# A fused long convolution and token MLP on one core: the filter's transposes into 16-bit PSUM, and another fixed order

## The chip, the core and the metric

The kernel runs on one core of one Trainium2 chip. The metric is the device time of one execution in microseconds; the times shown are medians of several runs. A profile is one execution recorded by the hardware, with its own time.

## What is computed

The reference, cut to what matters (D = 640 channels, S = 2048 steps, F = 1536; all tensors bf16):

```python
def _A_ref(q, k, v, shift_k, ssm_k, ssm_D):          # long convolution
    k_shift = sum of k shifted by 0..3 steps, times shift_k per channel
    kv = k_shift * v
    y = causal convolution of kv with ssm_k along S   # by FFT of length 2S
    y = y + kv * ssm_D
    return q * y
def _B_ref(x, w1, b1, w2, b2):                        # MLP over the steps
    u = gelu(einsum("bsd,sf->bdf", layernorm(x), w1) + b1)
    return transpose(einsum("bdf,fs->bds", u, w2) + b2)
g = sigmoid((q * gate_w).sum(-1))
return g * _A_ref(...) + (1 - g) * _B_ref(q, ...)
```

## The kernel before

**The work.** The convolution is done with matrices of cosines and sines. The filter `ssm` is five blocks of 128 channels by 2048 steps; it is loaded block by block (`db` = 0 to 4). For each half `h` of the steps and each block, `transp` (L798) transposes eight 128x128 pieces on TensorE, by multiplying with the identity `ident`, into one PSUM slot, and one instruction copies the slot, scaled by 1/1024, into `wT`. So there are ten such blocks of eight transposes. For `h` = 0, GpSimd first adds the channel's `ssm_D` to the filter's first step (L803). Then `wblock` (L818) multiplies `wT` with the tables FE, FN and FO into the filter's spectrum: two groups of 16 matmuls of 128 columns per block, each group evacuated by one instruction ("Wb") into C. FE and FN are computed on the core; FO is loaded in two tables of 256 KB (p = 1 and p = 3). For `h` = 1 every group reads both FO tables; for `h` = 0 one of the two groups reads them.

Beside that, `x_load` brings q (as X) in pieces; VectorE takes its statistics (L897), GpSimd works out the reciprocal deviation (L902), and ScalarE or VectorE normalizes X in 16 instructions (L911). k is permuted by VectorE (`k_turn`, L702) and transposed by DMA into KT, multiplied by the shift filter KF on TensorE ("kv"), and by v on VectorE. Then come the spectrum of kv ("A"), the first MLP matmul ("m1", 12 tiles of four groups of eight matmuls of 320 columns, reading X and the weights in `ring`), the products of the spectra on VectorE, the second MLP matmul ("m2", reading GT and W2), and the inverse transform ("inv", reading C or SS and GTB). The last TensorE group is an m2 group; two VectorE instructions (L627) and an output DMA follow it.

**PSUM slots.** There are four slots (`pp`) of 1024 float32 per partition. Each group of matmuls has one, and the group that gets the slot next has to wait for its evacuation. The kernel's own tracker (class `_Tracker`) writes a semaphore wait for every overlap of memory.

**The order.** Every operation has a number in the order in which the code creates it (0 to 648). `_ORDER` (L1318) lists all numbers in the order in which they are issued; each engine's queue is that list cut to its own operations, and each engine works strictly in that order. `_ENG` (L1342) has one letter for each of the 50 operations that may go to ScalarE ("A") or VectorE ("D"): for each block one wT and two Wb, the 16 normalizations, and the four permutations of k. `_SLOTS` (L1343) gives the PSUM slot of each group. Nothing of that is worked out when the kernel runs.

The numbers that are used below:

| number | operation |
|---|---|
| 2; 5 | load of filter block 0, first half; second half |
| 6, 7, 8, 9 | loads of filter blocks 1 to 4, 512 KB each |
| 3, 4 | load of X, first 512 rows: 160 KB and 480 KB |
| 12, 13, 14 | loads of the other three parts of X, 640 KB each |
| 10, 11 | loads of the two FO tables, 256 KB each |
| 15, 16, 17 | small loads of b2 and b1 |
| 18, 19, 45, 46 | loads of W1's first third, by part of the rows |
| 43, 44 | loads of k, first half |
| 36, 38 | ScalarE: the sine of the tables; a gelu of one element that brings the gelu table |
| 60, 67, 74, 81, 88 | GpSimd: addition of `ssm_D` for blocks 0 to 4 |
| 61, 68, 75, 82, 89 | TensorE: transposes for h = 0, blocks 0 to 4; the evacuations are 62, 69, 76, 83, 90 |
| 197, 203, 209, 215, 221 | the same for h = 1; the evacuations are 198, 204, 210, 216, 222 |
| 63, 70, 77, 84, 91 and 65, 72, 79, 86, 93 | TensorE: spectrum groups of h = 0 without and with FO |
| 199 to 225 in steps (199, 201, 205, 207, ...) | TensorE: spectrum groups of h = 1 |
| 53 to 59 | TensorE: dummy pairs of matmuls on zeros (`zz`), 512 columns |
| 131 to 134, 152 to 155, 173 to 180 | normalizations of X, four per part |
| 181 to 184 | GpSimd: the four products that make KF |
| 186, 188, 241, 243 | SP: DMA transposes of k |
| 405 | ScalarE: the gelu of the fifth m1 tile |
| 482, 483, 484, 501 | loads into W2 where m2 groups have read it (483 waits for 479, its first user is 519) |
| 611, 612 | VectorE: the last two operations that write SS |

The queues around the change, before. SP: 13, 6, 2, 7, 10, 11, 14, 17, 8, 12, 4, 44, 9, 43, 3, 5, 18, then the DMA transposes 188 and 186. TensorE: 55, 53, 57, 59, 56, the small constants (48), 54, then 203, 68, 58, 61, 209, 75, 207, 65, 79, 72, 211, 82, and so on. ScalarE: the sine, then evacuations; 38 stands behind 405. VectorE takes wT of 61 and 75 (62 and 76) and two of the Wb.

Of the kernel before, what the change touches and what calls it, by code (L numbers as in the profile page):

```python
# [9 lines left out]
BF16 = mybir.dt.bfloat16  # L10
# [9 lines left out]
class _Tracker:  # L20
# [265 lines left out]
    def mm(self, ps_ap, lhsT, rhs, start, stop, final_val, inc, transpose=False):  # L286
        acc_r = []
        for a in (lhsT, rhs):
            for r in self.regions(a):
                acc_r.append((r, "R"))  # L290
        acc = list(acc_r)
        ps_regs = self.regions(ps_ap)
        if start:
            for r in ps_regs:
                acc.append((r, "W"))
        need = self.deps_for("PE", acc)
        self.do_waits("PE", need)
        ins = self.nc.tensor.matmul(ps_ap, lhsT=lhsT, rhs=rhs, start=start, stop=stop, skip_group_check=True)  # L298
        src = ("eng", "PE", final_val)
        for reg, mode in acc_r:  # L300
            self.add_record(reg, "R", src)
        for r in ps_regs:
            self.add_record(r, "W", src)
        if inc:
            ins.then_inc(self.clk["PE"], 1)
            self.cnt["PE"] += 1
            assert self.cnt["PE"] == final_val, (self.cnt["PE"], final_val)
            self.hist["PE"].append(dict(self.known["PE"]))
        return ins
# [123 lines left out]
def _build(nc, A_q, A_k, A_v, A_shift_k, A_ssm_k, A_ssm_D, B_x, B_w1, B_b1, B_w2, B_b2, gate_w, out):  # L433
    Bsz, S, D = A_q.shape
# [5 lines left out]
    SL = 4 * D  # L440
# [3 lines left out]
    with ExitStack() as es:  # L444
        clk = {e: es.enter_context(nc.semaphore(f"clk_{e}")) for e in ENGS}
        T = _Tracker(nc, clk)

        pp = []
        for i in range(4):
            h = es.enter_context(nc.psum_tensor(f"pp{i}", [128, 1024], F32))  # L450
# [7 lines left out]
        def alloc(name, shape, dtype, at=None):  # L458
            size = mybir.dt.size(dtype)
            for s_ in shape[1:]:  # L460
                size *= s_
            if at is None:
                off = cur[0]
                cur[0] = (off + size + 63) // 64 * 64
            else:
                off = at
            assert off % 4 == 0 and off + size <= top, f"SBUF overflow {name}: {off}+{size} > {top}"
            h = nc.alloc_sbuf_tensor_at(name, list(shape), dtype, offset=off)
            T.reg_sbuf(h, off)
            return h  # L470

        def base_of(h):
            return T.mem[h.name][1]

        def V(h, off, dims, p0=0, pn=128):
            row = T.mem[h.name][2]
            return bass.AP(tensor=h, offset=p0 * row + off, ap=[[row, pn]] + [list(d) for d in dims])

        gwb = alloc("gwb", [128, D], BF16)
        ident = alloc("ident", [128, 128], BF16)  # L480
# [40 lines left out]
        ssm = alloc("ssm", [128, ND, S], BF16, at=base_of(C[3]))  # L521
        wT = alloc("wT", [128, 4, 4, D], BF16, at=base_of(C[2]))
# [82 lines left out]
        def either(name, o, i, rd, on_act, on_dve, vt=None):  # L605
            e_ = {"A": "ACT", "D": "DVE"}[next(which)]

            def emit(s):
                src = i(s) if vt is not None else i
                return T.op(e_, lambda e: (on_act if e_ == "ACT" else on_dve)(e, src), rd + [src], [o])  # L610
            return SC.add(e_, act_dur(n_of(o)) if e_ == "ACT" else dve_dur(n_of(o), 1), emit, rd if vt is not None else rd + [i], [o], vt=vt, name=name)

        def evac(name, o, i, vt, scale=1.0):
            kw = {} if scale == 1.0 else {"scale": scale}
            return either(name, o, i, [], lambda e, src: e.activation(o, src, ACT.Copy, **kw),  # L615
                          lambda e, src: e.tensor_copy(o, src) if scale == 1.0 else e.tensor_scalar(o, src, scale, None, op0=ALU.mult), vt=vt)
# [18 lines left out]
        def memset(eng, ap, val, prio=None):  # L635
            return nolock(eng, 0.2, lambda s: T.op(eng, lambda e: e.memset(ap, val), [], [ap]), [], [ap], prio=prio)

        def mms(vt, items, prio=None, name="mm"):
            dur = sum(max(n_of(r) / 2400.0 + 0.0025, 0.056) for _, _, r, _, _ in items)
            rd = []  # L640
            for _, l, r, _, _ in items:
                rd += [l, r]

            def emit(s):
                fv = T.cnt["PE"] + 1
                for k_, (o, l, r, st, sp) in enumerate(items):
                    T.mm(o(s), l, r, st, sp, fv, k_ == len(items) - 1)
            return SC.add("PE", dur, emit, rd, [], prio=prio, vt=vt, name=name)

        ndma = [0]  # L650
# [129 lines left out]
        vt = _VT("cv")  # L780
        items = []
# [16 lines left out]
        def transp(h, db):  # L798
            vt = _VT("cv")
            items = []  # L800
            if h == 0:
                w0 = V(ssm, db * S, [[1, 1]])
                tt("POOL", w0, w0, dcol[:, db:db + 1], ALU.add)  # L803
            for j in range(7, -1, -1):
                items.append(((lambda s, j=j: s[:, 128 * j:128 * j + 128]), V(ssm, db * S + 1024 * h + j, [[8, 128]]), ident[:, :], True, True))
            m_ = mms(vt, items, name="wtr")
            evac("wT", V(wT, 2 * h * SL + 128 * db, [[SL, 2], [D, 4], [1, 128]]), (lambda s: s[:, :].rearrange("q (a b c) -> q a b c", a=2, b=4)), vt, 1.0 / 1024.0)

        def table(p, kt, c, k2):
            if p % 2:  # L810
# [245 lines left out]
        for ft in range(FT):  # L1056
# [3 lines left out]
            vt = _VT("mlp")  # L1060
            r = ring[(ft // 4) % 2]
            col = 128 * (ft % 4)
            for hk in range(4):
                items = []
# [43 lines left out]
        for hk, p in [(hk, p) for hk in range(2) for p in range(4)] + [(hk, p) for p in INVP[1] for hk in (2, 3)]:  # L1108
            for a in {(1, 0): (4, 6, 8), (2, INVP[1][0]): (10,)}.get((hk, p), ()):
                w2_pair(a)  # L1110
            vt = _VT("mlp")
# [4 lines left out]
            for a in range(na):  # L1116
                items = []
# [198 lines left out]


_ORDER = """  # L1318
# [22 lines left out]
"""  # L1341
_ENG = "DAAAAADDAAAAAADDDDDAAADDDADDDDADDAAAAAAAAAAAAAAADD"  # L1342
_SLOTS = "1120021323201331122022011133001030332021001010110220110131230121002123231321103301332230032032101133201012203121332133113300113"  # L1343
# [1 line left out]
_INS = ['A_q', 'A_k', 'A_v', 'A_shift_k', 'A_ssm_k', 'A_ssm_D', 'B_x', 'B_w1', 'B_b1', 'B_w2', 'B_b2', 'gate_w']  # L1345
_OUTS = [((1, 2048, 640), 'bfloat16')]
# [23 lines left out]
```

## Time and profile before

| what | us |
|---|---|
| median of 3 runs | 176.82 (176.80 to 177.04) |
| the profiled execution, its own time | 177.12 |
| its span, first to last instruction | 175.1 |
| TensorE (PE) matmuls busy | 170.0 |
| VectorE (DVE) busy | 168.9 |
| ScalarE (ACT) busy | 107.6 |

The page gives busy time per engine, then the span in 40 slices of 4.4 us, where each digit is the busy share of a slice in tenths. PEclk is the granted share of TensorE's clock. PEld is TensorE's loading of weights, which overlaps the matmuls. A row of a group reads: line, engine, operation, output <- inputs, shape, count, then busy time in us, mean of one in ns, and the idle time of the engine just before them with what ended it. A row of a timeline reads: start in us, length in us, engine, line, operation, output <- inputs, count, and in brackets the idle time before it and who ended it. SPq and POOLq are the DMA queues of SyncE and GpSimd; "to landing" is the time from a DMA's issue to its last byte. Matmuls overlap, so the time per matmul is read from start to start, not from the length of one. A row of stretches reads: the stretch, its length, busy time (and count) of PE, PEld, DVE, ACT and POOL, the granted clock, the DMA share and the GB/s.

### The profile page before, as it was taken

How to read it: one execution, taken by the hardware profiler on the slowest of the kernel's cores; microseconds unless marked ns; L12 is line 12 of the kernel's file. 1: busy time of each engine (PE TensorE's matmuls, PEld its weight loads, DVE VectorE, ACT ScalarE, POOL GpSimd, SP SyncE). 2: the span in 40 equal slices, each digit the busy share in tenths (PEclk: the TensorE clock that was granted, in tenths of full speed). 3: DMA queues.
4: the chain of work that ended last, by engine and by line, in shares of the span. 5: the costliest groups of instructions: out<-in, count | busy, mean ns of one | idle time of the engine just before them, and what ended most of it. 6: DMA issues, size and time to landing. Idle time of an engine off the chain costs nothing.

```text
span 175.1 us, 3683 instructions
## 1 busy us (share of the span) xinstructions
PE 170.0 (97%) x1559; PEld 138.2 (79%) x1559; DVE 168.9 (96%) x187; ACT 107.6 (61%) x160; POOL 42.7 (24%) x62
## 2 busy tenths in 40 slices
PE   7999999999899999999999999999999999999992
PEld 2599999877697767777777778888899998698782
DVE  7899999999999999999999999999999999999984
ACT  4499999997999997877556214222215105645760
POOL 3199891000000650003202202220055000052200
PEclk9999999999999999999999999999999999999999
DMA  5999999999999799992999999999939999549598
GB/s 144 397 421 405 376 200 225 380 375 221 179 383 356 172 192 192 186 358 57 178 174 365 353 211 349 282 207 240 300 108 187 197 177 372 241 65 209 106 233 292
DMA packets 33248, 44.06 MB, mean 252 GB/s; under 512 B 12112, under 2 KB 24656, under 8 KB 33104
## 3 DMA queue, kind: packets, MB, share of 16 engines
q1 hardware_dynamic: 28024, 32.68, 57.6%
q0 software_dynamic: 5168, 11.14, 37.4%
q8 instruction: 12, 0.20, 0.4%
q14 instruction: 4, 0.03, 0.1%
q10 hardware_dynamic: 40, 0.01, 0.0%
HBM read 27.44 MB, written 2.62 MB: 172 GB/s over the span
## 4 chain that ended last, share of the span: by engine, by line
PE 93%; DMA 3%; ACT 2%; DVE 0%; DVEq 0%; SPq 0%; issue 0%
PE pp L298 93%; DMA ssm<-in_A_ssm_k_dram 3%; ACT L600 1%; ACT ksh L600 1%; ACT GT L600 0%; DVE O L627 0%; DVEq L426 0%; SPq L272 0%
## 5 line engine op out<-in xcount | busy, mean ns | idle before, releaser
L298 PE MATMUL pp<-X,ring 128*128 128x320 bf16 x384 | 55.4, 299 | 0.5 <-ACT GT L600 0.5
L556 DVE TENSOR_TENSOR C<-C 128x2560 bf16<-128x2560 bf16 (+2 forms) x38 | 54.6, 1485 | 0.3 <-ACT C L600 0.2
L298 PE MATMUL pp<-GT,W 128*128 128x320 bf16 x384 | 53.6, 299 | 0.0
L298 PEld LDWEIGHTS pp<-GT,W 128*128 128x128 bf16 x384 | 48.0, 129 | 4.6
L298 PEld LDWEIGHTS pp<-X,ring 128*128 128x128 bf16 x384 | 37.0, 98 | 15.0 <-ACT GT L600 0.8
L600 ACT ACTIVATE O<-pp,c,omg 128x640 bf16<-128x640 f32 x15 | 12.9, 883 | 24.8 <-PE pp L298 24.8
L267 POOL DMA_DIRECT2D C<-C x8 | 10.5, 1674 | 51.1 <-DVE C L556 30.0
L600 ACT ACTIVATE C<-pp 128x640 bf16<-128x640 f32 x32 | 20.4, 711 | 2.0 <-PE pp L298 2.0
L600 ACT ACTIVATE cgb<-pp,gg 128x640 bf16<-128x640 f32 x16 | 12.1, 795 | 13.3 <-PE pp L298 7.6
L615 ACT ACTIVATE C<-pp 128x1024 bf16<-128x1024 f32 x18 | 17.1, 1051 | 0.3 <-PE pp L298 0.3
L600 ACT ACTIVATE gq<-gq 128x640 bf16<-128x640 bf16 x16 | 11.6, 727 | 5.7 <-DVE gq L556 5.7
L556 DVE TENSOR_TENSOR tm<-C,C 128x5120 bf16<-128x5120 bf16 x5 | 14.1, 2819 | 0.1
L897 DVE BATCH_NORM_STATS2 stats<-X 128x6 f32<-128x320 bf16 x32 | 13.1, 470 | 0.4 <-DMA X<-in_A_q_dram 0.2
L298 PE MATMUL pp<-wT,FO 128*128 128x128 bf16 x160 | 12.4, 219 | 0.0
L600 ACT ACTIVATE GT<-pp,cc 128x640 bf16<-128x640 f32 x12 | 9.3, 793 | 4.8 <-PE pp L298 4.7
L298 PE MATMUL pp<-C,GTB 128*128 128x320 bf16 x80 | 11.9, 299 | 0.0
L298 PE MATMUL pp<-wT,FE 128*128 128x128 bf16 x120 | 11.7, 219 | 0.0
L556 DVE TENSOR_TENSOR SS<-C 128x2560 bf16<-128x2560 bf16 x8 | 11.7, 1482 | 0.0
L267 POOL DMA_DIRECT2D O<-q_hi x4 | 4.8, 1324 | 27.7 <-DVE q_hi L556 27.7
L600 ACT ACTIVATE ksh<-pp 128x1024 bf16<-128x1024 f32 (+1 forms) x12 | 10.1, 908 | 1.4 <-PE pp L298 1.3
L267 POOL DMA_DIRECT2D C<-q_hi x4 | 4.8, 1198 | 23.8 <-DVE q_hi L556 10.9
L556 DVE TENSOR_TENSOR C<-tm 128x2560 bf16<-128x2560 bf16 x7 | 10.3, 1487 | 0.1
(92 smaller groups left out, 225.3 us busy)
## 6 DMA issues: line engine op xcount, KB each, us to landing
ring<-in_B_w_dram SPq DMA_DIRECT2D x12, 512.0 KB, 8.8
W<-in_B_w_dram SPq DMA_DIRECT2D x12, 512.0 KB, 6.8
C<-C POOLq DMA_DIRECT2D x8, 640.0 KB, 8.8
kn<-in_A_k_dram SPq DMA_DIRECT2D x4, 640.0 KB, 9.6
C<-q_hi POOLq DMA_DIRECT2D x4, 640.0 KB, 9.7
out_dram<-O SPq DMA_DIRECT2D x7, 320.0 KB, 3.2
ssm<-in_A_ssm_k_dram SPq DMA_DIRECT2D x4, 512.0 KB, 7.0
X<-in_A_q_dram SPq DMA_DIRECT2D x3, 640.0 KB, 7.3
```

What stands on the lines that cost most here:

```text
L267: ins = engobj.dma_start(out_ap, in_ap, accum_op=ALU.add, max_dma_last_dim=2560)
L298: ins = self.nc.tensor.matmul(ps_ap, lhsT=lhsT, rhs=rhs, start=start, stop=stop, skip_group_check=True)
L556: o_ = SC.add(eng, d, lambda s: T.op(eng, lambda e: e.tensor_tensor(o, a, b, op), rd, [o]), rd, [o], prio=prio, name="tt")
L600: return T.op("ACT", lambda e: e.activation(o, src, func, **kw), rr + [src], ww)
L615: return either(name, o, i, [], lambda e, src: e.activation(o, src, ACT.Copy, **kw), lambda e, src: e.tensor_copy(o, src) if scale == 1.0 ...
L897: ops.append(SC.add("DVE", 0.38, (lambda o, i: lambda s: T.op("DVE", lambda e: e.bn_stats(o, i), [i], [o]))(o, i), [i], [o]))
```

## The change

Three things change. First, the transposes are issued in TensorE's transpose form (`is_transpose`), and their output is written as bf16 into the first half of the slot instead of as float32 into all of it; the evacuation reads it as bf16. Second, `_ENG` gives other operations to VectorE: wT of 68, 89 and 197 (69, 90, 198) instead of 62 and 76, nine normalizations instead of eleven, and two Wb as before (92 and 214 instead of 78 and 94). Third, `_ORDER` and `_SLOTS` are new from end to end. In the new order SP issues 12, 6, 2, 7, 13, 8, 14, 4, 10, 11, 9, 5, 44, 3, 43, 17, 18, 19, then 188 and 186; TensorE goes 58, 53, 59, 55, 56, 48, 54, then 203, 61, 68, 57, 209, 75, 63, 70, 82, 77, 215, 84, 207, 217, 211, 89, 86, 65, 221, 197, 72, 205, 201, 91, 93, 79, and so on; 38 stands right behind 36 on ScalarE.

```diff
         need = self.deps_for("PE", acc)
         self.do_waits("PE", need)
-        ins = self.nc.tensor.matmul(ps_ap, lhsT=lhsT, rhs=rhs, start=start, stop=stop, skip_group_check=True)
+        ins = self.nc.tensor.matmul(ps_ap, lhsT=lhsT, rhs=rhs, start=start, stop=stop, skip_group_check=True, **({"is_transpose": True} if transpose else {}))
...
-        def mms(vt, items, prio=None, name="mm"):
+        def mms(vt, items, prio=None, name="mm", transpose=False):
...
-                    T.mm(o(s), l, r, st, sp, fv, k_ == len(items) - 1)
+                    T.mm(o(s), l, r, st, sp, fv, k_ == len(items) - 1, transpose)
...
             for j in range(7, -1, -1):
-                items.append(((lambda s, j=j: s[:, 128 * j:128 * j + 128]), V(ssm, db * S + 1024 * h + j, [[8, 128]]), ident[:, :], True, True))
-            m_ = mms(vt, items, name="wtr")
-            evac("wT", V(wT, 2 * h * SL + 128 * db, [[SL, 2], [D, 4], [1, 128]]), (lambda s: s[:, :].rearrange("q (a b c) -> q a b c", a=2, b=4)), vt, 1.0 / 1024.0)
+                items.append(((lambda s, j=j: s[:, 64 * j:64 * j + 64].bitcast(BF16)), V(ssm, db * S + 1024 * h + j, [[8, 128]]), ident[:, :], True, True))
+            m_ = mms(vt, items, name="wtr", transpose=True)
+            evac("wT", V(wT, 2 * h * SL + 128 * db, [[SL, 2], [D, 4], [1, 128]]), (lambda s: s[:, 0:512].bitcast(BF16).rearrange("q (a b c) -> q a b c", a=2, b=4)), vt, 1.0 / 1024.0)
...
-_ENG = "DAAAAADDAAAAAADDDDDAAADDDADDDDADDAAAAAAAAAAAAAAADD"
+_ENG = "AAADAAAAAAAADDADDAADDDDDADDAAAADDDAAAAAAADAAAAAADD"
-_SLOTS = "1120021323201331122022011133001030332021001010110220110131230121002123231321103301332230032032101133201012203121332133113300113"
+_SLOTS = "1123020201110022333022012033103321113030300332311313200003131123201303300332031012002121033213031202331213200321323013131201012"
```

The 16 lines of `_ORDER` are left out; the parts of it that matter here are told above.

44 rows, old and new, of the table _ORDER are left out of this document.

## The prediction

> **What bounds the kernel now.** I read the page first, then the chain of waits in order of time, then the timelines of TensorE, VectorE, ScalarE and the SP queue. The page's busy rows:
>
> ```profile
> PE 170.0 (97%) x1559; PEld 138.2 (79%) x1559; DVE 168.9 (96%) x187; ACT 107.6 (61%) x160; POOL 42.7 (24%) x62
> ACT  4499999997999997877556214222215105645760
> PEclk9999999999999999999999999999999999999999
> ```
>
> TensorE and VectorE are both full; ScalarE is full in slices 2 to 9, about 9 to 44 us, where the change sits. The chain, in order of time (start, length):
>
> ```profile
> 1.19 5.37 DMA ssm<-in_A_ssm_k_dram
> 6.60 27.17 PE pp L298 x443
> 33.78 7.29 PE pp L298 x88
> 41.09 1.02 ACT ksh L600
> 42.13 1.28 ACT L600
> 43.43 0.81 ACT GT L600
> 44.28 127.63 PE pp L298 x988
> ```
>
> After the first filter load, TensorE runs to 171.9 us almost without a break. So I price everything by how far it delays TensorE's stream. Three stretches show its pace and its gaps:
>
> ```profile
> 10.27 3.07 PE L298 MATMUL pp<-wT,FO 128*128 128x128 bf16 x52
> 13.18 0.33 PE L298 MATMUL pp<-wT,FE 128*128 128x128 bf16 x3
> ...
> 24.74 1.21 PE L298 MATMUL pp<-ident,ssm 128*128 128x128 bf16 x16
> 25.79 0.33 PE L298 MATMUL pp<-wT,FE 128*128 128x128 bf16 x3
> ...
> 30.26 1.25 PE L298 MATMUL pp<-X,ring 128*128 128x320 bf16 x8
> ...
> 32.52 1.25 PE L298 MATMUL pp<-X,ring 128*128 128x320 bf16 x8
> 33.78 1.75 PE L298 MATMUL pp<-KF,KT 128*128 128x128 bf16 x32
> ```
> ```profile
> 40.89 1.25 PE L298 MATMUL pp<-X,ring 128*128 128x320 bf16 x8
> 41.98 0.71 PE L298 MATMUL pp<-vkv,FE 128*128 128x320 bf16 x4
> 42.52 1.25 PE L298 MATMUL pp<-X,ring 128*128 128x320 bf16 x8
> 44.28 1.26 PE L298 MATMUL pp<-X,ring 128*128 128x320 bf16 x8 [0.51 <-ACT GT L600]
> ```
>
> Start to start, a filter-spectrum matmul takes (13.18-10.27)/52 = 56 ns, so a group of 16 takes 0.89 us; a transpose (25.79-24.74)/16 = 66 ns, a block of eight 0.53; eight of 320 columns take 1.09 (40.89 to 41.98). Eight of these took 1.26 at 32.52 and 1.76 at 42.52: gaps of 0.17 and 0.67 us, behind ScalarE (the last chain rows: an evacuation, a table load, a gelu). VectorE is as tight near the end:
>
> ```profile
> 161.20 2.88 DVE L556 TENSOR_TENSOR SS<-C 128x2560 bf16<-128x2560 bf16 x2
> ```
> ```profile
> 164.12 4.51 PE L298 MATMUL pp<-SS,GTB 128*128 128x320 bf16 x32
> ```
>
> VectorE finishes SS at 164.08; TensorE needs it at 164.12. A gain therefore has to be had on both.
>
> **The change, part by part.**
>
> *Evacuations.* The rows that price them (view by shapes; the fourth is a 16-bit operation of 1024 elements per partition that reads SBUF):
>
> ```profile
> L615 ACT ACTIVATE wT<-pp 128x1024 bf16<-128x1024 f32 x8 | 8.1, 1042 | 1.1 <-PE pp L298 1.1
> L616 DVE TENSOR_SCALAR wT<-pp 128x1024 bf16<-128x1024 f32 x2 | 2.4, 1182 | 0.0
> L915 DVE TENSOR_SCALAR X<-X,rstd,nb 128x640 bf16<-128x640 bf16 x11 | 4.3, 434 | 0.0
> L570 DVE TENSOR_SCALAR pint<-pint 128x1024 int16<-128x1024 int16 x1 | 0.4, 428 | 0.0
> ```
>
> Read letter by letter, the new engine string gives VectorE three of the ten wT evacuations (two before), nine of the sixteen normalizations (eleven before), and again two of the twenty Wb. An evacuation from 16-bit PSUM is not in the trace. On VectorE it lies between 428 and 1182 ns; I take 0.7 us, between the two, as it shares the element type with the one row and the source with the other. VectorE's sum is then 3 x 0.7 - 2 x 1.18 - 2 x 0.43 = -1.1 us (+0.3 at the upper end). On ScalarE I leave 1042. [...]
>
> *ScalarE.* It loses a wT evacuation and gains two normalizations, and the second table load moves from behind op 405's place in the list to right behind the sine:
>
> ```profile
> 5.93 0.18 ACT L600 ACTIVATE dcol<-pp 128x5 bf16<-128x5 f32 x1 [1.20 <-PE pp L298]
> ...
> 27.32 4.70 ACT L615 ACTIVATE C<-pp 128x1024 bf16<-128x1024 f32 x5
> ...
> 34.03 1.79 ACT L914 ACTIVATE X<-X,nb,rstd 128x640 bf16<-128x640 bf16 x2
> ```
>
> In a row, an evacuation costs (4.70-1.05)/4 = 0.91 us and a normalization 1.79-0.98 = 0.81. So ScalarE reaches the first gelu 0.91 - 1.62 + 1.28 = 0.57 us sooner. The load falls into the 1.20 us for which ScalarE idles before 5.93; with its one-element gelu it exceeds that by 0.3 us, hidden because the filter load lands later (6.56). The gaps of 0.17 and 0.67 go: **-0.84 us**. What could be late next there is op 133, a normalization that the first MLP group needs. It stands behind 23 evacuations and one normalization: 23 x 0.91 + 2 x 0.81 = 22.6 us after the first evacuation can start (7.1, after eight transposes), so 29.7 at the least, while TensorE comes at 6.60 + 23.66 (as before, 30.26 - 6.60) + 0.53 (below) = 30.8. That hides it.
>
> *The transposes on TensorE.* 80 instructions of unchanged size. Their 66 ns against 56 may vanish (-0.8 us in all) or grow by as much; nothing in the trace decides, so zero, and 0.8 to both sides.
>
> *First transposes.* Before, the order was 203, 68, a dummy pair, then 61; now 61 comes second. 61 needs GpSimd's addition into block 0:
>
> ```profile
> 7.28 0.20 POOL L556 TENSOR_TENSOR ssm<-ssm,dcol 128x1 bf16<-128x1 bf16 x1 [0.33 <-DMA ssm<-in_A_ssm_k_dram]
> ```
>
> That ends at 7.48, and the load before it keeps its place (third, same bytes ahead). TensorE is there at 6.60 + 0.53 = 7.13: **+0.38 us**, with 68 and the dummies queued behind it.
>
> *The FO tables.* SP issued them fifth and sixth; now they are ninth and tenth, behind two more pieces of X of 640 KB, one of 480 KB and one more filter block. Issue rows, then the time from issue to landing of FO, of the 640 KB piece of X issued at 5.51 and of the 480 KB piece issued at 5.99:
>
> ```profile
> 2.75 1.30 SPq L272 DMA_DIRECT2D FO<-odd_tab  x2
> ...
> 5.51 0.96 SPq L272 DMA_DIRECT2D X<-in_A_q_dram  x2
> ```
> ```profile
> DMA to landing us min/median/max: 6.4/6.4/6.4
> ```
> ```profile
> DMA to landing us min/median/max: 8.8/8.8/8.8
> ```
> ```profile
> DMA to landing us min/median/max: 10.7/10.7/10.7
> ```
>
> Before, FO landed at 9.2 and 9.9. In the new order 4704 KB are in the queue up to the second table; the old order has the same big transfers up to the X piece that landed at 5.99 + 10.7 = 16.7 us. The 640 KB piece, with 4224 KB, landed at 14.3; the remaining 480 KB at the stretch's 406 GB/s would give 15.5:
>
> ```profile
> 4.00:14.00 10.00, 9.82 (x135) 7.95 (x134) 8.95 (x25) 7.34 (x10) 5.83 (x9) 1.00 1.02 406
> ```
>
> So the second table lands between 15.5 and 16.7. I take 16.3, near the row with the same bytes, less some for the small load of b1 that no longer stands ahead. Who needs it: group 207, the thirteenth from the first transpose in the new TensorE list. Ahead of it stand seven transposes (7 x 0.53), one dummy pair (0.43) and four spectrum groups (4 x 0.89): 6.60 + 7.7 + 0.38 = 14.7. Its last four matmuls read the second table at 14.7 + 12 x 0.056 = 15.3. **+1.0 us** (0.2 to 1.4), and all of TensorE's queue is behind it; ScalarE has evacuations in stock then, but runs dry later and cannot give it back.
>
> *Smaller waits.* By the new list and 0.91 us per evacuation TensorE meets a slot that is still being read, or the fifth block's addition behind the four KF products, a few times by under 0.1 us: **+0.15**.
>
> *The rest of the order* I cost at nothing: each later SP load has 11 us or more of TensorE work between its last reader and its first user, more than most landings of W, but for one (a rival below). SP's transposes of k and the v loads behind them start later by about the same as their users.
>
> Sum: -0.84 + 0.38 + 1.0 + 0.15 = **+0.7 us**. VectorE, 1.1 us ahead, does not bind; the tail behind TensorE's last group is unchanged. The profiled execution took 177.12 us (span 175.1 and 2.0 around it), 0.3 above the median of 176.82. So 176.82 + 0.7 = **177.5 us**.
>
> **The rivals.**
>
> *Not slower: FO lands in time.* The term decides from 15.3 us on; at 15.5 the sum falls to -0.1, **176.7**. For it: the steady 406 GB/s. Against: the last piece of the same set took until 16.7.
>
> *Faster: the transposes shed their 10 ns*, and FO lands early: -0.1 - 0.8 at best, **175.9 to 176.4**. For it: only transposes, with their strided weights, run above 56 ns. Against: the weights stay strided, and part of the gain would fall into waits for ScalarE.
>
> *Slower: VectorE gets nothing from 16 bits* (1.18 us). Place: op 198, the third of its evacuations, which 201 needs. VectorE comes to it behind 31 of the 32 statistics, a copy of k and two evacuations; I put its end at about 23 us with 0.7 each and 24.4 with 1.18, against TensorE's 23.8 with the waits above. It decides from about 1.0 us per evacuation; a further +0.5 to 1.2, **178.0 to 178.7**.
>
> [...]
>
> *A W2 load comes late.* Load 483 waits for 479, and 519 needs it six groups later, 6 x 1.09 = 6.5 us; the least room before was 10.9. Landings of all W loads, and of the one issued alone at 116.5 us:
>
> ```profile
> DMA to landing us min/median/max: 3.8/6.8/11.3
> ```
> ```profile
> DMA to landing us min/median/max: 4.7/4.7/4.7
> ```
>
> Up to +1 at the median with its issue, **178.5**; 483 would be issued nearly alone, and 4.7 hides it.
>
> **Chances.** Forecast (+0.2 to +1.4) 0.46; FO in time 0.18; faster 0.16; VectorE slow 0.09; clock 0.04; W2 or another load 0.07. About 0.2% (0.35 us) is what a measurement of this kernel tells from no change. Of FO in time 0.05 is faster by more than that, and 0.08 of the forecast lies within it: faster 0.21, same 0.21, slower 0.58. The range, 176.1 to 178.9, takes in both ends of the FO term, half of the transposes' 0.8 and the slow VectorE; the forecast's own is 177.0 to 178.2.
>
> **What would show it.** Right: a TensorE gap near 15 us released by FO, a smaller one at 7.1 by GpSimd's addition, no gap at 42 to 44, a table load before 6 us, wT evacuations on VectorE near 0.7 us. Wrong: no wait for FO; transposes at another pace; TensorE's MLP starting before 30.8 us; a granted clock below 1.0; gaps after 45 us.

## The result, and the profile after

The changed kernel took 178.73 us (median of 4 runs, 178.41 to 178.80), the kernel before 176.93 on the same chip: a ratio of 1.0093 (95% interval 1.0081 to 1.0105), 1.8 us slower. The forecast was 177.5 with a range of 176.1 to 178.9, and slower as the likeliest. The profiled execution of after took 178.74 us (before 177.12).

The page of after: busy time, then two of its rows of 40 slices.

```profile
PE 169.4 (96%) x1559; PEld 138.2 (78%) x1559; DVE 167.8 (95%) x186; ACT 109.4 (62%) x161; POOL 41.8 (24%) x62
PE   6996999999999999999999999999999999999992
PEclk9999999999999999999999999999999999999999
```

TensorE now has a hole in its fourth slice (13.2 to 17.7 us); the granted clock is 9 (90% or more) in every slice and 1.00 as the mean of each of the four runs. VectorE has 1.1 us less work than before, which is what the forecast said, and it did not help. The chain of after in order of time (start, length; short pieces left out):

```profile
4.85 11.64 DMA FO<-odd_tab
...
16.54 85.86 PE pp L298 x893
...
102.41 0.02 SPq L199
...
102.46 0.37 SPq L272
...
104.89 7.57 DMA W<-in_B_w_dram
...
112.51 55.63 PE pp L298 x408
```

Before, TensorE ran from 6.6 us to the end with one break near 43. Now the end hangs on two loads: FO, and a W2 load behind SP. The timeline of TensorE has both, and a third, smaller wait near 7:

```profile
7.07 1.20 PE L298 MATMUL pp<-ident,ssm 128*128 128x128 bf16 x16 [0.24 <-DMA ssm<-in_A_ssm_k_dram]
...
14.56 0.22 PE L298 MATMUL pp<-wT,FN 128*128 128x128 bf16 x1
16.54 0.40 PE L298 MATMUL pp<-wT,FO 128*128 128x128 bf16 x4 [1.76 <-DMA FO<-odd_tab]
...
21.35 1.17 PE L298 MATMUL pp<-ident,ssm 128*128 128x128 bf16 x16
22.35 1.06 PE L298 MATMUL pp<-wT,FO 128*128 128x128 bf16 x16
...
32.39 3.42 PE L298 MATMUL pp<-X,ring 128*128 128x320 bf16 x24
...
109.82 2.34 PE L298 MATMUL pp<-GT,W 128*128 128x320 bf16 x16
112.51 1.69 PE L298 MATMUL pp<-GT,W 128*128 128x320 bf16 x11 [0.35 <-DMA W<-in_B_w_dram]
```

Start to start, and less the matmul itself, the waits are 0.41 us at 6.6, 0.26 at 11.3 (filter block 3), 1.92 at 14.6 (FO) and 0.51 at 111.9 (W2). The gaps of 0.17 and 0.67 us behind ScalarE are gone. For the larger the reason is the table load, which stands early now (first line). The smaller had another: before, it ended with an evacuation into `ksh`, which stands ahead of the table load in ScalarE's queue (second line, TensorE's weight loads before).

```profile
5.34 1.28 ACT L600 ACT_TABLE_LOAD   x1
```
```profile
33.77 1.59 PEld L298 LDWEIGHTS pp<-KF,KT 128*128 128x128 bf16 x32 [0.34 <-ACT ksh L600]
```

A book with two entries holds it all. The first MLP matmul starts at 32.39 us (before 30.26): the start lost **2.13**. From there to TensorE's last matmul (173.56, before 171.90) it is 141.17 us (before 141.64): the rest gained **0.47**. Together that is 1.66, and the profiled executions differ by 1.62.

### The profile page after: what moved, and what is told of

Same layout as the page of the kernel before. It is cut to its first block, busy times and chain, and to the rows that moved or that the text cites. A ratio compares the mean times of both kernels' runs of the same rounds, so it can differ in the third digit from the quotient of the medians.

```text
span 176.8 us, 3679 instructions
## 1 busy us (share of the span) xinstructions
PE 169.4 (96%) x1559; PEld 138.2 (78%) x1559; DVE 167.8 (95%) x186; ACT 109.4 (62%) x161; POOL 41.8 (24%) x62
## 3 DMA queue, kind: packets, MB, share of 16 engines
HBM read 27.44 MB, written 2.62 MB: 170 GB/s over the span
## 4 chain that ended last, share of the span: by engine, by line
PE 80%; DMA 11%; SPq 3%; DVE 2%; ACT 1%; issue 0%; DVEq 0%
PE pp L298 80%; DMA FO<-odd_tab 7%; DMA W<-in_B_w_dram 4%; SPq L272 3%; DVE O L556 1%; DVE cgb L556 1%; ACT cgb L600 1%; DVE O L627 0%; DVEq L426 0%; DVE cgb L570 0%; SPq L199 0%
## 5 line engine op out<-in xcount | busy, mean ns | idle before, releaser
L600 ACT ACTIVATE O<-pp,c,omg 128x640 bf16<-128x640 f32 x15 | 13.2, 884 | 31.2 <-PE pp L298 31.2
L615 ACT ACTIVATE C<-pp 128x1024 bf16<-128x1024 f32 x18 | 17.7, 1025 | 1.6 <-PE pp L298 1.6
L897 DVE BATCH_NORM_STATS2 stats<-X 128x6 f32<-128x320 bf16 x32 | 13.7, 466 | 1.1 <-DMA X<-in_A_q_dram 1.1
L267 POOL DMA_DIRECT2D C<-SS x3 | 5.3, 1768 | 37.0 <-DVE C L556 37.0
L298 PEld LDWEIGHTS pp<-wT,FO 128*128 128x128 bf16 x160 | 9.8, 98 | 2.0 <-DMA FO<-odd_tab 1.9
L556 DVE TENSOR_TENSOR C<-tm 128x2560 bf16<-128x2560 bf16 x7 | 10.3, 1488 | 0.1
```

What stands on the lines that cost most here:

```text
L267: ins = engobj.dma_start(out_ap, in_ap, accum_op=ALU.add, max_dma_last_dim=2560)
L556: o_ = SC.add(eng, d, lambda s: T.op(eng, lambda e: e.tensor_tensor(o, a, b, op), rd, [o]), rd, [o], prio=prio, name="tt")
L600: return T.op("ACT", lambda e: e.activation(o, src, func, **kw), rr + [src], ww)
L897: ops.append(SC.add("DVE", 0.38, (lambda o, i: lambda s: T.op("DVE", lambda e: e.bn_stats(o, i), [i], [o]))(o, i), [i], [o]))
```

## The experiments

Each ratio is to the kernel before, run on the same chip, where its median was 176.89 to 177.31 us; the changed kernel's is 1.0093, and comparisons with the changed kernel go by these ratios. "SP" lines are the order of the loads in SP's queue.

### FO ahead of two pieces of X

```diff
 SP: 12 6 2 7 13 8
+10 11
 14 4
-10 11
 9 5 44
```

> Only the two FO loads move: on SP they go from ninth and tenth to seventh and eighth, ahead of two pieces of X (640 and 480 KB). Theory (FO's place in the queue makes the 1.92 us gap before group 207): the FO tables land near 12.5 us, two full pieces sooner, and the gap goes. But TensorE then reaches the fifth filter block's transposes (op 89), four groups later, at about 17.3 us, and block 4 still lands at 18.3: a new gap of about 1.0 us, so a gain of about 0.9 us against the changed kernel, near 177.8. Rival (the whole gap is recovered or kept elsewhere, because TensorE is held by ScalarE or VectorE later anyway): less than 0.3 us of gain, and the lost time shows as PSUM-slot waits after 20 us.

Measured: 179.43 us, ratio 1.0143 (1.0124 to 1.0162). FO landed at 12.5 and 13.1 and no group waits for it. TensorE, then two lines of VectorE:

```profile
18.64 0.71 PE L298 MATMUL pp<-ident,ssm 128*128 128x128 bf16 x8 [1.12 <-DMA ssm<-in_A_ssm_k_dram]
...
22.49 0.69 PE L298 MATMUL pp<-ident,ssm 128*128 128x128 bf16 x8 [0.87 <-DVE wT L616]
```
```profile
14.72 1.28 DVE L897 BATCH_NORM_STATS2 stats<-X 128x6 f32<-128x320 bf16 x3 [1.30 <-DMA X<-in_A_q_dram]
...
17.34 2.06 DVE L897 BATCH_NORM_STATS2 stats<-X 128x6 f32<-128x320 bf16 x5 [0.88 <-DMA X<-in_A_q_dram]
...
21.71 0.64 DVE L616 TENSOR_SCALAR wT<-pp 128x1024 bf16<-128x1024 bf16 x1
```

The new wait for block 4 came as expected (1.28 us start to start). Neither theory had the second one: VectorE waits twice for the pieces of X, so its evacuation of wT, queued behind 29 of the 32 statistics, is late, and TensorE waits another 1.03 us for the slot. Giving evacuations to VectorE tied TensorE to the arrival of X. The first MLP matmul starts at 33.33, later than in the changed kernel.

### FO and block 4 ahead

```diff
 SP: 12 6 2 7 13 8
+10 11
 14
+9
 4
-10 11 9
 5 44
```

> As the run before, and filter block 4 goes ahead of the 480 KB piece of X as well. Theory (each load's place decides): neither FO nor block 4 is waited for by more than 0.3 us, the gain against the changed kernel is 1.5 to 1.9 us, near 177.0. Rival (the pieces of X, now 0.75 to 1.25 MB later, make the statistics and normalizations late): TensorE's first MLP group or the DMA transposes of k wait, and less than 1.0 us is gained.

Measured: 181.69 us, ratio 1.0253 (1.0213 to 1.0293). The rival's direction, and far more than either had. TensorE's wait, and then the stretches (length; busy PE, PEld, DVE, ACT, POOL; granted clock; DMA share; GB/s):

```profile
23.55 0.73 PE L298 MATMUL pp<-ident,ssm 128*128 128x128 bf16 x5 [2.70 <-DVE wT L616]
```
```profile
22.00:23.00 1.00, 0.00 (x0) 0.00 (x0) 1.00 (x7) 0.72 (x1) 0.68 (x3) 1.00 1.08 342
23.00:24.00 1.00, 0.45 (x5) 0.48 (x6) 1.00 (x3) 0.00 (x0) 0.93 (x2) 0.79 0.49 144
24.00:25.00 1.00, 1.00 (x12) 1.00 (x11) 1.00 (x3) 0.00 (x0) 0.99 (x3) 0.50 0.17 58
...
27.00:28.00 1.00, 1.00 (x21) 1.00 (x19) 1.00 (x5) 0.36 (x1) 0.67 (x4) 1.00 1.18 218
```

TensorE now waits 2.87 us for the same evacuation, and after that pause its clock is 0.50 until 27 us: 12 matmuls per us in place of 21. Of the six runs, four have a mean clock of 0.99 (181.4 to 182.4 us) and two of 1.00 (180.0 and 180.4). So neither of the two other orders of these loads that were tried suits this order of work: FO later starves TensorE, X later starves VectorE and through it TensorE. Not all of that is the order's, though. Each of the two traces also has one load that lands over 1 us later than its bytes explain: in the first the 480 KB of X, 2.62 us behind the piece ahead of it (1.23 in the changed kernel), in the second block 4, 2.52 us behind the load ahead of it (1.29). The last experiment says what goes together with that.

### W2 load 464 behind the others

```diff
 SP: 458
-464
 459 462 460 461
+464
 465 463
```

> In the changed kernel load 464 stands second among the W2 loads on SP, waits until 102.4 us for the MLP group 443 and holds 459, 462, 460 and 461 behind it, whose own buffers are free 8 to 15 us earlier. Here 464 alone moves behind 461. Theory (the queue's head holds the others up): 459 to 461 are issued between 88 and 97 us, the wait of 0.51 us at 112.5 goes, the gain is 0.4 to 0.6 us, near 178.2. Rival (what ends the kernel is VectorE's SS by then, not TensorE): the wait goes and the time stays within 0.15 us.

Measured: 179.72 us, ratio 1.0162 (1.0141 to 1.0184): slower than the changed kernel. 459 was issued at 85.3, but 462 stood behind the MLP group 441 until 97.3, with 460 and 461 behind it, so these were issued at 97.3 to 99.1 us. That is 6 to 7 us sooner than in the changed kernel and not the 8 to 17 expected, and it is the time of another load. VectorE, then the load of q_hi that it waits for (KB, us to landing) here and in the changed kernel, then TensorE:

```profile
107.44 1.49 DVE L556 TENSOR_TENSOR q_hi<-C,SS 128x2560 bf16<-128x2560 bf16 x1 [2.09 <-DMA C<-q_hi]
```
```profile
C<-q_hi POOLq DMA_DIRECT2D x1, 640.0 KB, 10.3
```
```profile
C<-q_hi POOLq DMA_DIRECT2D x1, 640.0 KB, 7.6
```
```profile
116.04 2.20 PE L298 MATMUL pp<-GT,W 128*128 128x320 bf16 x15 [0.33 <-ACT O L600]
```

The wait for W2 went. But GpSimd's load, with the W2 loads now under way beside it, took 2.7 us longer. VectorE lost 2.1 us, the small operation behind it that ScalarE needs was late, and TensorE waited 0.49 us for ScalarE's evacuation and, between 145 and 167 us, another 1.0 us, nearly all of it for VectorE. The cause of the wait for W2 was not told apart by this run; the last experiment does it.

### The 16 bits alone

The kernel before with only the transposes' form and their 16-bit output.

```diff
 (kernel before: its _ORDER, _ENG and _SLOTS)
-m_ = mms(vt, items, name="wtr")
+m_ = mms(vt, items, name="wtr", transpose=True)
 (output and evacuation as bf16, as in the change)
```

> The kernel before with its own order, engines and slots, and the transposes in TensorE's transpose form into 16-bit PSUM alone. Theory (the order costs the time, the 16 bits next to nothing): VectorE's two evacuations take 0.65 us instead of 1.18, the transposes run 62 to 66 ns apart as before, the two gaps of 0.17 and 0.67 us behind ScalarE stay, and the time is within 0.3 us of the kernel before, near 176.8. Rival (the 16-bit transposes themselves cost time, by pace or by a slower clock): slower by 0.5 us or more, with the transposes over 70 ns apart or a granted clock below 1.0.

Measured: 177.01 us, ratio 1.0005 (0.9983 to 1.0028), as the theory had it. The groups by shapes: this kernel, the changed one (mean ns behind the comma):

```profile
L615 ACT ACTIVATE wT<-pp 128x1024 bf16<-128x1024 bf16 x8 | 8.1, 1043 | 1.2 <-PE pp L298 1.2
L616 DVE TENSOR_SCALAR wT<-pp 128x1024 bf16<-128x1024 bf16 x2 | 1.3, 666 | 0.4 <-PE pp L298 0.4
```
```profile
L615 ACT ACTIVATE wT<-pp 128x1024 bf16<-128x1024 bf16 x7 | 7.0, 1027 | 0.5 <-PE pp L298 0.5
L616 DVE TENSOR_SCALAR wT<-pp 128x1024 bf16<-128x1024 bf16 x3 | 2.0, 674 | 0.7 <-PE pp L298 0.7
```

VectorE's evacuation falls from 1182 to 666 and 674 ns, ScalarE's stays (1042, 1043, 1027), and the clock is 1.00. The microsecond that VectorE gains turns into waits for X (0.85 us) and for TensorE (0.42).

### The order alone

The changed kernel without the 16 bits: plain matmuls into float32, everything else new.

```diff
 (changed kernel: its _ORDER, _ENG and _SLOTS)
-m_ = mms(vt, items, name="wtr", transpose=True)
+m_ = mms(vt, items, name="wtr")
 (output and evacuation as float32, as before)
```

> The changed kernel's order, slots and engines with the transposes as plain matmuls into float32, so the order alone. Theory (the order costs the time, and VectorE is as tight as TensorE): VectorE's three evacuations take 1.18 us instead of 0.66, 1.6 us in all, of which some falls into its waits for TensorE between 19 and 26 us; 0.3 to 1.2 us slower than the changed kernel, 179.0 to 179.9, a ratio to before of 1.012 to 1.017. Rival (the 16 bits are worth nothing here either): within 0.25 us of the changed kernel, a ratio of 1.008 to 1.011.

Measured: 178.60 us, ratio 1.0065 (1.0044 to 1.0086), no slower than the changed kernel. The theory falls in its second half: VectorE's evacuations take 1.22 us again, and TensorE waits for them 0.16 us at 9.9, ahead of its wait for FO, and 0.06 at 24.2; the end is no later for it. The order costs the time. And this trace shows FO's wait in another shape:

```profile
15.00 0.40 PE L298 MATMUL pp<-wT,FO 128*128 128x128 bf16 x4 [0.15 <-DMA FO<-odd_tab]
...
17.07 0.40 PE L298 MATMUL pp<-wT,FO 128*128 128x128 bf16 x4 [1.45 <-DMA FO<-odd_tab]
```

The first table is nearly in time here and the second comes 2.07 us behind it; in the changed kernel the first was late. Start to start the two waits are 0.31 and 1.61, 1.92 again.

### The early table load alone

```diff
 ACT: 36
+38
 49 50 ...
 405
-38
```

> The kernel before, with only op 38 (the gelu that brings the table) moved right behind the sine. Theory (VectorE is tied with TensorE at the end, SS at 164.08 against 164.12): TensorE's gaps of 0.17 and 0.67 us go, VectorE gains nothing, new waits of TensorE for SS or C show late, and the gain is 0.3 us at most, 176.5 to 176.9. Rival (TensorE's gaps are all that counts): 0.7 to 0.85 us faster, near 176.1.

Measured: 177.06 us, ratio 0.9983 (0.9957 to 1.0009), which, as a ratio, both the theory's range and no change allow. The trace decides against the theory's reason: the two gaps are gone (0.84 us) and nothing waits for SS or C in their place. 0.41 us of it went at 8.4 (0.25, filter block 2 landed at 8.69, before 8.53) and at 25.5 (0.16); TensorE ends at 171.43, 0.47 sooner. The gap of 0.17 is gone because of these delays: TensorE comes to it 0.4 us later, and the evacuation into `ksh` that ended it is done 0.2 later. VectorE finishes SS within 0.1 us of TensorE's need again, but does not hold it up.

### 16 bits and early table, then one normalization to ScalarE

```diff
 (16 bits, and 38 behind 36, with the order of before)
```

> The kernel before with the 16-bit transposes and the table load right behind the sine: what both engines need, without the new order. Theory (both bounds have to move): VectorE has 1.06 us less, of which 0.85 fell into a wait for X and 0.2 at 40 us in the run with the 16 bits alone, TensorE 0.84 less; 0.2 to 0.6 us faster than before, 176.3 to 176.7. Rival (TensorE alone counts): 0.75 to 0.9 us faster, near 176.0; rival (VectorE's stream from 18 us on is solid): no gain.

Measured: 176.69 us, ratio 0.9978 (0.9954 to 1.0002); TensorE ends at 171.38. That is the theory's size, though the interval just allows no change, but not its reason: the larger gap is gone (below), the one of 0.17 at 33.6 is not, and no wait for VectorE stands in their place.

```profile
42.68 2.34 PE L298 MATMUL pp<-X,ring 128*128 128x320 bf16 x16
```

```diff
 (as above)
-_ENG: 177 "D"    ACT: ... 175 261 180 258
+_ENG: 177 "A"    ACT: ... 175 261 180 177 258
```

> As the run before, and one normalization (op 177, 0.36 to 0.43 us on VectorE) goes to ScalarE behind op 180, where the table load has made room (1.28 us less, 0.81 more). Theory (VectorE sets the end once TensorE's gaps are gone): a further 0.3 to 0.4 us, 175.9 to 176.4, 0.5 to 0.9 us faster than before. Rival (TensorE sets it): the same as the run before within 0.15 us.

Measured: 176.62 us, ratio 0.9966 (0.9942 to 0.9991); TensorE ends at 171.27. It is the one kernel here whose interval lies wholly below the kernel before, by 0.3%. The step from the run before, 0.1 us, is less than these intervals can tell, so the normalization proves nothing on VectorE.

### The two orders crossed

```diff
+order = before[:first MLP group] + [i for i in after if i is not in it]
```

> A cross of the two orders: everything that the kernel before issues ahead of its first MLP group (214 operations, with its engines and slots) and then the changed kernel's order for all others; 16-bit transposes, the table load behind the sine. Theory (the changed kernel loses in its start, and later only the 0.51 us for W2): as the kernel of before with 16 bits and the early table load, plus 0.5 us, a ratio to before of 0.999 to 1.003, with the wait for W2 near 110 us still there. Rival (the late part of the new order loses more, or VectorE's): a ratio of 1.006 or more.

```diff
+order = after[:first MLP group] + [i for i in before if i is not in it]
```

> The other cross: the changed kernel's first 216 operations, ahead of its first MLP group, and then the order, engines and slots of before. Theory (the start loses): the gap for FO near 15 us is there, the wait for W2 is not; 0.3 to 0.6 us faster than the changed kernel, a ratio of 1.006 to 1.008. Rival (the start's loss is absorbed later): a ratio under 1.003.

Measured: 177.81 us, ratio 1.0028 (1.0008 to 1.0048), and 179.39 us, ratio 1.0113 (1.0086 to 1.0140). Both got a wait where the halves meet that neither parent has, 1.40 us start to start in the first (first line) and 1.36 in the second (last line). The second also waits longer for block 0, 1.17 us at 6.8:

```profile
33.76 1.26 PE L298 MATMUL pp<-X,ring 128*128 128x320 bf16 x8 [1.23 <-DMA ring<-in_B_w_dram]
```
```profile
7.97 1.19 PE L298 MATMUL pp<-ident,ssm 128*128 128x128 bf16 x16 [1.01 <-DMA ssm<-in_A_ssm_k_dram]
...
34.43 1.34 PE L298 MATMUL pp<-KF,KT 128*128 128x128 bf16 x24 [1.20 <-ACT C L615]
```

So as sums they are inconclusive. What they keep: with the start of before, the first MLP matmul starts at 30.19, with the new start at 31.84, and the wait for W2 is absent from both, even from the first, where it was expected. There load 460 stands where it stood in the changed kernel, but it lands 7.1 us after its issue instead of 7.6, just as its first user comes: half a microsecond decides on this wait.

### Three groups that do not read FO

Groups 207, 217 and 211 read FE in the place of FO, so their part of the spectrum is another one; the loads are unchanged.

```diff
-items.append((..., table(p, kt, c, k2), ...))
+items.append((..., FE[:, p // 2, kt, c, :] if p % 2 and group in (207, 217, 211) else table(p, kt, c, k2), ...))
```

> The changed kernel, with groups 207, 217 and 211 reading FE in the place of FO, so that these three spectrum groups are computed with other data and wait for no FO table; all loads and queues as they are. Theory (filter block 4, landing at 18.3, is late next): the gap of 1.92 us at 14.6 goes, TensorE runs three groups (2.7 us) to 17.3 and waits 1.0 to 1.1 us there before the transposes 89; 0.8 us faster than the changed kernel, a ratio of 1.004 to 1.006. Rival (the FO wait is the whole loss): 1.7 to 1.9 us faster, a ratio of 0.998 to 1.000.

Measured: 177.84 us, ratio 1.0023 (1.0007 to 1.0039). The theory held, in the place and the size of the new wait (1.11 us start to start):

```profile
16.97 0.39 PE L298 MATMUL pp<-wT,FE 128*128 128x128 bf16 x4
18.31 0.71 PE L298 MATMUL pp<-ident,ssm 128*128 128x128 bf16 x8 [0.95 <-DMA ssm<-in_A_ssm_k_dram]
```

The wait of 1.92 us is worth 0.6 us at TensorE's end (172.96), 1.2 by the two ratios (about 0.9 to 1.6): block 4 was next.

### Load 460 before 462

```diff
 SP: 458 464 459
+460
 462
-460
 461 465 463
```

> The changed kernel with W2 load 460 moved two places up on SP, behind 459 and so still behind 464 only if 459 is; the order is 458, 464, 459, 460, 462, 461. Theory (464 at the queue's head is the cause, all loads behind it start at 102.4): 460 lands third in place of fourth, about 1.5 us sooner (111.0), just ahead of its first user at 112.0, and the wait of 0.51 us goes; 462, at 112.5, has its first user later. 0.3 to 0.5 us faster than the changed kernel, a ratio of 1.006 to 1.008. Rival (any change among these loads disturbs the loads that VectorE waits for): VectorE waits over 0.5 us near 105 us and nothing is gained.

Measured: 178.00 us, ratio 1.0029 (1.0014 to 1.0045). The wait for W2 is gone, the first line, and VectorE does not wait near 105 us. The other two lines are of the start, in which no load and no operation has another place than in the changed kernel:

```profile
108.75 5.46 PE L298 MATMUL pp<-GT,W 128*128 128x320 bf16 x39
```
```profile
14.84 0.40 PE L298 MATMUL pp<-wT,FO 128*128 128x128 bf16 x4
...
17.99 0.70 PE L298 MATMUL pp<-ident,ssm 128*128 128x128 bf16 x8 [0.30 <-DMA ssm<-in_A_ssm_k_dram]
```

(In the changed list 460 stood fifth, behind 464, 459 and 462; all four are issued in a row once 464 is free.) So 460's place in the row behind 464 was the cause, and one place up mends it: 460 lands at 109.73, 1.3 us ahead of its first user. But the kernel gained 1.1 us by the ratios (about 0.8 to 1.5), twice what the W2 wait was worth. FO was nearly in time, with waits of 0.08 and 0.21 us in place of 1.92. Why, with the same start? The transfers of 14.2 to 14.58, 14.58 to 14.78 and 14.78 to 16.0 us give a hint. First the changed kernel's first stretch, then the second stretch of the kernel with the order alone, then the third of this one (packets, MB, share of 16 engines); behind each, the time from issue to landing of its FO tables:

```profile
q1 hardware_dynamic: 77, 0.16, 105.7%
q8 instruction: 1, 0.02, 17.5%
```
```profile
DMA to landing us min/median/max: 11.6/11.6/11.6
```
```profile
q1 hardware_dynamic: 28, 0.08, 98.8%
q8 instruction: 1, 0.02, 32.8%
```
```profile
DMA to landing us min/median/max: 10.1/10.8/11.6
```
```profile
q1 hardware_dynamic: 150, 0.47, 99.2%
q8 instruction: 1, 0.02, 5.5%
```
```profile
DMA to landing us min/median/max: 9.9/10.0/10.1
```

Each has one packet of 16 KB of instructions that takes about 1.07 us of one engine's time (17.5% of 16 engines over 0.38 us; 5.5% over 1.22), while the data take nearly all of the 16. By the packet records it begins at 14.36, 14.59 and 14.79 us. In the table, with the other three traces that have this start, the load that lands late behind it is bold:

| kernel | packet | 480 KB of X | FO, first | FO, second | block 4 | first MLP |
|---|---|---|---|---|---|---|
| changed | 14.36 | 14.34 | **16.49** | 17.00 | 18.29 | 32.39 |
| order alone | 14.59 | 14.29 | 14.95 | **17.02** | 18.30 | 32.47 |
| this one | 14.79 | 14.11 | 14.79 | 15.46 | **17.94** | 31.32 |
| 464 moved | 14.91 | 14.71 | 15.40 | 16.06 | **17.79** | 31.46 |
| three groups without FO | 14.51 | 14.35 | 15.03 | **16.97** | 18.26 | 31.67 |
| second cross | 15.16 | 15.19 | 15.82 | 16.45 | 17.83 | 31.84 |

Without it a 256 KB table lands 0.5 to 0.7 us behind the load ahead of it and block 4 1.3 to 1.4; with it 1.94 to 2.15, and 2.48 and 1.73: 0.4 to 1.5 us more. Why the load is late is not shown: the moment of the packet was not steered in an experiment, the records do not name the DMA engine, and the last row has the packet with no load over 0.1 us late. The table shows that packet and late load go together in five of six traces with one start. Every other trace has such a packet too, at 13.8 to 14.8 us, and one late load behind it: the two orders with FO ahead (above), and the six traces that start as the kernel before, where the 480 KB of X land 2.1 to 2.6 us behind the piece ahead of them instead of 1.2.

## Why the prediction was right, and which terms were off

The sign and the mechanism were right, the size was short by 1.2 us, and part of the agreement is luck (see FO); the forecast's own range ended at 178.2. Going through its steps:

- **Evacuations.** VectorE was taken at 0.7 us and took 0.674; ScalarE was left at 1042 ns and took 1027. That VectorE does not bind was right: the order alone gives it 1.6 us more and ends no later.
- **The table load.** -0.84 was right in size, and for 0.67 of it in reason. The smaller gap ended with an evacuation that stands ahead of the table load, so its going was not the load's doing: with the order of before it stayed in one of three kernels with the early load, and 0.47 to 0.62 us reached TensorE's end.
- **The transposes.** Zero was right: 62.5 ns in the changed kernel (21.35 to 22.35 us, 16 of them), 60 to 66 as plain matmuls before. The slower clock, 0.04, is a term that no run shows: with these 80 transposes among the other matmuls the mean clock is 1.00 in all four runs.
- **The first transposes.** +0.38 measured 0.41, by another releaser: the half of block 0 itself landed at 7.03, so the group could not start; the addition, done at 7.39, was needed only by its last matmul.
- **Small waits.** +0.15 measured 0.26, all for block 3, a load that the step did not list.
- **FO.** "So the second table lands between 15.5 and 16.7. I take 16.3" failed: 17.00, and the first table, taken to be in time, at 16.49. The 16.7 was read as what the bytes need, but its load was late itself, behind a packet of instructions (at 14.14 us in the trace of before); in the changed kernel the first table was the late one. The gap was 1.92 instead of 1.0. Where the packet goes together with a late block 4 instead, or with no late load, the same start has waits for FO of 0.29, 0.49 and 0.60 us. So the bytes ahead of FO explain a wait, but not 1.0 us of it, and that the term came between the two cases is luck. Yet what it cost in the end was less, 0.6 us in the trace and 1.2 by the ratios, because block 4 is late next; the step did not ask what would be late next once this wait goes.
- **The start** began with 0.43 us that the sum did not have: the first X piece and block 1 landed 0.6 us sooner. It is not a steady gain: the first transposes start at 6.17 here, and at 6.16 to 7.36 in the other traces whose loads begin in this order, later where TensorE's first matmuls are slow for longer: with the order alone three dummies take 0.48 us each up to 6.14 us and the transposes start at 6.88, here dummies take 0.22 us each from 5.72 us on.
- **"The rest of the order I cost at nothing"** failed: 0.51 us. The room of each load was counted from its own last reader. Load 460 had its buffer free at about 89 us and was issued at 104.9, because 464 stood ahead of it on SP and waited until 102.4 for group 443. The rival for W2 named load 483 and the wrong mechanism.

By the two entries: the start was forecast at +1.53 (0.38, 1.0, 0.15) and lost 2.13; the rest at -0.84 and gained 0.47. The waits at the start add up to that loss: 0.41 + 0.26 + 1.92 - 0.43 = 2.16. The two entries together miss by 0.97 of the 1.2 us; most of the remainder is that the medians differ by 1.80 and the profiled executions by 1.62.

What stays open: whether the changed kernel's other runs have the packet at FO too. Its four times lie within 0.4 us of the profiled one; those of the last experiment's kernel spread over 1.1 us (177.19 to 178.26), about what the packet is worth.

## What to carry to other kernels

A load's room is counted on the queue that issues it: from the last wait of anything ahead of it there, not from its own buffer, and a load sent sooner is charged to whatever load is then under way for another engine (here 640 KB took 10.3 us in place of 7.6). Where the first loads fill the DMA engines (here a mean share of 1.00 from 4 to 14 us), price an order by the landing of every load that its groups need, one behind the other, and give a wait only the distance to the next late load (the 1.92 us for FO were worth 0.6 at TensorE's end); an engine's work that stands behind such a load in its queue (here an evacuation behind statistics of X) makes that load a need of its consumers too.

## What the runs showed of the hardware

- **Packets of instructions travel beside the data.** There are twelve packets of 16 KB in the changed kernel's span, 0.9 to 1.4 us each; in the start, at a DMA share of 1.00 from 4 to 14 us, one of them goes together with a landing 0.4 to 1.5 us late, in 13 of 14 traces. That the packet makes the load late is the author's guess; no run shows it.
- **After a pause of 2.87 us TensorE's clock was halved** for about 3.4 us in the profile of the second experiment: TensorE is idle from 20.84 to 23.55 us, and the granted clock is 0.79 from 23 to 24 us, 0.50 from 24 to 27 and 1.00 from 27 to 30. The mean clock of that run is 0.99, as in three more of its six runs. After the 1.92 us in the changed kernel (idle from 14.78 to 16.54) the clock stayed at 1.00. How long a pause has to be is not shown.
- **16-bit PSUM instead of float32 made VectorE's evacuation of wT shorter, not ScalarE's:** 1182 to 674 ns on VectorE, 1042 to 1027 on ScalarE for the same 1024 elements.
